# Loads of q, k pair by pair through a tile of four places, v in parts, and turning transfers behind x's transpositions

## The chip, the cores and the metric

The kernel runs on one core of one Trainium2 chip. The metric is the device time of one execution in microseconds. The core has five engines that run side by side, each in the order of its own program: TensorE (PE, with its weight loads PEld), VectorE (DVE), ScalarE (ACT), GpSimd (POOL) and SyncE (SP). SP only issues DMAs here; POOL issues all loads from HBM that change float32 into bfloat16. All DMAs run on the core's 16 DMA engines.

## The reference

Eight batches, eight heads, 576 positions, head size 64. First an attention with a decay, then a mixer along the sequence and one along the channels:

```python
scores = scale * q @ k.T                       # per batch and head, 576 x 576
cum    = cumsum(max(s, 0))
scores = where(causal, -1e9, scores + minimum(-(cum_i - cum_j), 0))
attn   = exp(scores - max) / (sum + 1e-9)
x      = (attn @ v), heads side by side        # 8 x 576 x 512
u      = x + (x.T @ U @ V).T                   # U: 576 x 32, V: 32 x 576
out    = u + max(u @ w_ch1, 0) @ w_ch2         # 512 -> 2048 -> 512
```

Inputs and output are float32; the kernel multiplies in bfloat16.

## The kernel before

**Tiling.** The 64 heads are worked in 32 pairs of heads (n = 0 to 31), four pairs to a batch (b, hp = divmod(n, 4)). For a pair the kernel needs q and k with the head size on the partitions, in a tile `slot` (one of three for the later pairs, so pair n takes over the slot of pair n - 3). `scores` multiplies k by q for the blocks on and below the diagonal into PSUM, ACT takes the exponential into a tile `pT`, DVE masks it. `values` multiplies pT by v (a column of ones beside v gives the sums), and DVE divides and writes `x_sb` (L502, L503). When the four pairs of a batch are there, `seqmix` makes u from x: products with U and V, to which DVE adds x transposed (`xT`, L547). Then `chanmix` takes 512 rows of u at a time: `hidden` (L662, ReLU by ACT at L1039) and `outputs_by_quarters` (L720), which uses a scheme of seven products in place of eight, with sums made by DVE (L698, L734).

**How q and k come.** For batches 0 to 3 (b < ZB = 4) q and k are loaded in one or a few transfers and PE transposes them (`transposes`, L322). For batches 4 to 7 the DMA transposes them: `load_pairs(b)` issues 16 loads (L121) into one of two tiles `qk_sd`, by batch in turns; `turn_pair(n)` (L358) is a transposing DMA on SP's queue that writes one of three landing places; `part_pair(n)` brings the decay rows in by two small DMAs (`rows_of`, L302) and lets DVE copy the landing into the slot (L366). `values` sends each finished pair of x to `xT` by a transposing DMA on SP as well (L510), and `by_token` does the same for u (`u_sd`, L1026). v goes by `load_v(b)` in five parts of 128 positions (the last of 64, L185) into one of the v tiles; a batch's tile is that of the batch two before it, so the load waits for the last `values` of that batch.

**The order.** A loop over n from 8 to 33, "step n" below, writes the program: loads, the turn of pair n + 3, `part_pair(n + 1)` or `transposes(n + 1)`, `scores(n)`, then `values(n - 1)`; in the second step of a batch the `seqmix` of the batch before is woven in, and in between `step_fill` puts pieces of `chanmix` at a given pace. PE and POOL keep exactly this order (the last line of the kernel ties each instruction to the one before). DVE, ACT and SP are ordered by the tile framework's scheduler after the start of the kernel, which may put an instruction ahead of where it was written: the copies of L366 stand on DVE two steps ahead of the scores that use them, right behind the scores that last used the slot, and before the change the turns stood ahead as well. Each engine then runs its own order and waits at each instruction for what it needs. POOL and SP are queues too: what waits at their head holds what is behind.

**PSUM.** Four buffers `pwork` rotate in the order of allocation between the hidden products, the output products, the tails of scores, the products of values and seqmix; two larger ones (`pscore`) take the scores. PE stops when the buffer that is next has not been read out.

Of the kernel before, what the change touches and what calls it, by code (L numbers as in the profile page):

```python
# [16 lines left out]
ALU = mybir.AluOpType  # L17


def in_program_order(tc, first, engines):  # L20

    traced, last = tc.nc.cur_bb.bb.instructions, {}
    for ins in list(traced)[first:]:
        if ins.engine not in engines:
            continue
        prev = last.get(ins.engine)
        if prev is not None:
            tc.add_manual_dep(
                ins,
                prev.name,  # L30
                mybir.DependencyInfo(
                    mybir.DependencyClass.NoSync, mybir.DependencyReason.DATA
                ),
                reason="in_program_order",
            )
        last[ins.engine] = ins


# [1 line left out]
def kernel(  # L40
# [12 lines left out]
    nc = tc.nc  # L53
    traced = len(nc.cur_bb.bb.instructions)
    E = mybir.EngineType
    B, H, S, D = q.shape
# [7 lines left out]
    NP = BH // 2  # L64
    PB = NP // B
# [5 lines left out]
    ZB = 4  # L71
    TR, RT = 96, 6
# [12 lines left out]
    def pwork():  # L85
        return ps_w.tile([128, 512], FP32, tag="w", name="pwork")
# [17 lines left out]
    qk_sd = [consts.tile([128, 2 * H * TT * D], BF16, name=f"qk_sd{i}") for i in range(2)]  # L104
    QK = 2 * PB * RT * 128
# [1 line left out]
    def alloc_qk(b):  # L107
        q_t[b], k_t[b] = qk_sd[b % 2][:TP].rearrange("p (c h x) -> c p h x", c=2, h=H)

    def by_pairs(b):  # L110
        return qk_sd[b % 2][:TR, :QK].rearrange(
            "p (hp c t two d) -> p hp c t two d", hp=PB, c=2, t=RT, two=2
        )

    def in_runs(b, h):
        return b > 2 or b == 2 and h >= 4

    def load_pairs(b):
        for h in range(H):
            for c, src in enumerate((q, k)):  # L120
                nc.gpsimd.dma_start(  # L121
                    out=by_pairs(b)[:, h // 2, c, :, h % 2, :],
                    in_=src[b, h].rearrange("(t p) d -> p t d", p=TR),
                )

    def load_qk(b, h, n):
# [44 lines left out]
    def init_v(eng, vt):  # L171
        eng.memset(vt[64:, 4, :, :], 0.0)
        eng.memset(vt[:, 0:4, :, D : D + 1], 1.0)
        eng.memset(vt[0:64, 4, :, D : D + 1], 1.0)

    def v_slot(b):
        return v_slots[b % 3 if b < 3 else 2 - b % 2]

    def load_v(b, parts=range(5)):
        vt = v_slot(b)  # L180
        if 0 < b < 3:
            init_v(nc.gpsimd, vt)
        for t in parts:
            rows_t = 128 if t < 4 else 64
            nc.gpsimd.dma_start(  # L185
                out=vt[:rows_t, t, :, 0:D],
                in_=v[b, :, ds(t * 128, rows_t), :].rearrange("h p d -> p h d"),
            )
# [40 lines left out]
    for n in range(PB):  # L229
        for hh in range(2):  # L230
            nc.sync.dma_start(
                out=slots[n][D:KA, hh, 0 : 2 * S],
                in_=rows[2 * n + hh : 2 * n + hh + 1].rearrange("n r c s -> n r (c s)"),
# [3 lines left out]
    for r, n_r, c in ((0, 3, 1), (3, 1, 0)):  # L237
        nc.sync.dma_start(
            out=rows_hbm[ds(r, n_r), ds(2 * PB, BH - 2 * PB)].rearrange("r n s -> n r s"),
            in_=rows[2 * PB :, ds(r, n_r), c, :],  # L240
# [107 lines left out]
            yield  # L348

    landings = [consts.tile([128, 2 * S], BF16, name="turned")]  # L350
    landings += [qk_sd[(ZB + i) % 2][:, ds(QK, 2 * S)] for i in range(2)]

    def landing(n):
        return landings[(n - ZB * PB) % 3]

    def turn_pair(n):
        b, hp = divmod(n, PB)
        nc.sync.dma_start_transpose(  # L358
            out=landing(n).rearrange("p (a m) -> p a m", m=TR),
            in_=by_pairs(b)[:, hp].rearrange("p c t two d -> p (c t two d)"),  # L360
        )

    def part_pair(n):
        rows_of(n)
        for hh in range(2):
            nc.vector.tensor_copy(slot_of(n)[0:D, hh, 0 : 2 * S], landing(n)[ds(hh * D, D)])  # L366
            yield
# [113 lines left out]
    def values(n, pT):  # L481
        b, hp = divmod(n, PB)
        if hp == 0:
            x_of[b] = work.tile([128, PB, 5, 128], BF16, tag="x_sb", name="x_sb")
            if b >= FT:
                xT_of[b] = work.tile([128, 4, 640], BF16, tag="xT", name="xT", bufs=1)
        x_sb, vt = x_of[b], v_slot(b)
        for hh in range(2):
            h = 2 * hp + hh
            po = pwork()[:, : 5 * (D + 1)].rearrange("p (i d) -> p i d", i=5)  # L490
            for i in range(5):
                for j in range(i + 1):
                    nc.tensor.matmul(  # L493
                        po[:, i, :],
                        lhsT=pT[:, hh, ds(place(j, i), 128)],
                        rhs=vt[:, j, h, :],
                        start=(j == 0),
                        stop=(j == i),
                        skip_group_check=True,
                    )  # L500
            rec = work.tile([128, 5, 1], FP32, tag="rec", name="rec", bufs=4)
            nc.vector.reciprocal(rec, po[:, :, D : D + 1])  # L502
            nc.vector.tensor_tensor(  # L503
                x_sb[:, hp, :, ds(hh * D, D)],
                po[:, :, 0:D],
                rec.to_broadcast([128, 5, D]),
                op=ALU.mult,
            )
            if hh == 1 and b >= FT:
                nc.sync.dma_start_transpose(  # L510
                    out=xT_of[b][:, hp, :].rearrange("p (t m) -> p t m", t=5),
                    in_=x_sb[:, hp, :, :].rearrange("p t d -> p (t d)"),
                )
            yield


# [725 lines left out]
    for n in range(2 * PB, NP + 2):  # L1242
        b, hp = divmod(n, PB)
        if hp == 0 and b + 1 < ZB:
            load(b + 1)
        if hp == (1 if b >= ZB else PB - 1) and ZB <= b + 2 < B:
            load_pairs(b + 2)
        if ZB * PB <= n + 3 < NP:
            turn_pair(n + 3)
        mixing = seqmix(b - 1) if hp == 1 and b > FT else iter(())  # L1250
        if b == B:
            fill_with(3)
            for _ in range(3):
                step(mixing)
                fill_with(2)
        if n > 2 * PB and n + 1 < NP:
            for at, _ in enumerate((transposes if n + 1 < ZB * PB else part_pair)(n + 1)):
                step_fill()
                if at == 0:
                    step(mixing)  # L1260
        if 2 * PB + 1 < n < NP:
            for at, _ in enumerate(scores(n, pT_of(n))):
                step_fill()
                if at == 1:
                    step(mixing)
        for _ in mixing:
            fill_with(1)
        if hp == 1 and FT < b < B:
            fill.append(chanmix(b - 1))
            pace[1] = 12 if b < 6 else 10  # L1270
        if 2 * PB < n <= NP:
            run(values(n - 1, pT_of(n - 1)))
        if hp == 0 and 2 <= b < B - 1:
            load_v(b + 1)
    pace[1] = 16
    while NG - 3 not in expanded:
        step_fill()
# [67 lines left out]
```

## Time and profile before

| | us |
|---|---|
| median of three runs | 357.47 (356.61 to 358.28) |
| the profiled execution, its own time | 359.33 |
| its span in the profile | 357.6 |
| PE busy, idle | 343.6, 14.0 |
| DVE, ACT, POOL busy | 264.4, 207.6, 112.6 |

The granted clock of TensorE was full all through. Times in the views are counted from the start of the span. A line of a timeline gives start, duration (several instructions may be merged into one line), engine, line of the kernel, what is written from what is read, and in brackets the idle time of the engine before it with what ended that. SPq is SP's queue: its durations are those of issuing, not of the transfer. The end of a transfer is seen in the semaphore that it raises. In PE's idle time of 14.0 us, gaps of over 0.1 us add up to 9.2 us, 2.4 of it before 23 us.

| place | where in the loop | steps |
|---|---|---|
| 65 to 104 us | batch 2 | 9 to 12 |
| 104 to 142 us | batch 3 | 13 to 16 |
| 142 to 177 us | batch 4 | 17 to 20 |
| 177 to 213 us | batch 5 | 21 to 24 |
| 213 to 248 us | batch 6 | 25 to 28 |
| 248 to 282 us | batch 7 | 29 to 32 |

(A row runs from the end of the x of one batch, L503, to that of the next; step n ends with the values of pair n - 1.)

### The profile page before, as it was taken

The page shows a single profiled execution, that of the slowest core. Times are in us where ns is not written, and L with a number is a line of the kernel's source. Part 1 is how long each engine was busy: PE and PEld are TensorE (multiplying, and loading weights), DVE is VectorE, ACT ScalarE, POOL GpSimd, SP SyncE. Part 2 cuts the span into 40 slices and gives each one's busy share as a digit, 9 for nine tenths or more (in the row PEclk, how much of TensorE's full clock was granted, in tenths as well). Part 3 has the DMA queues.
Part 4 walks back from the last instruction along what each step waited for, and adds up shares of the span by engine and source line. Part 5 has one row for each costly group of instructions (what it writes and reads, how often), then busy time and mean ns, then how long its engine had stood idle before and what let it go on. Part 6 is the DMA issues. An engine that isn't in the chain of part 4 may idle for free.

```text
span 357.6 us, 9219 instructions
## 1 busy us (share of the span) xinstructions
PE 343.6 (96%) x3770; PEld 247.9 (69%) x3770; DVE 264.4 (74%) x584; ACT 207.6 (58%) x314; POOL 112.6 (31%) x158
## 2 busy tenths in 40 slices
PE   7999999999998999999999997899899999999996
PEld 3685656665587657775678565776588558888885
DVE  8686776779789849883798465983788779676774
ACT  4786965847762577348833874347752554675710
POOL 8897274447356603850366040000000000000000
PEclk9999999999999999999999999999999999999999
DMA  6999999999999999999599999472033525010022
GB/s 100 163 193 203 177 187 121 146 144 97 192 101 171 162 168 88 167 176 159 72 120 160 204 118 90 73 163 57 0 57 83 115 30 120 29 60 31 29 90 88
DMA packets 163713, 42.06 MB, mean 118 GB/s; under 512 B 148312, under 2 KB 162040, under 8 KB 163672
## 3 DMA queue, kind: packets, MB, share of 16 engines
q0 software_dynamic: 101744, 18.45, 80.7%
q1 hardware_dynamic: 61640, 22.83, 36.0%
q8 instruction: 29, 0.48, 0.6%
q10 hardware_dynamic: 288, 0.20, 0.2%
q14 instruction: 12, 0.10, 0.1%
HBM read 37.25 MB, written 9.70 MB: 131 GB/s over the span
## 4 chain that ended last, share of the span: by engine, by line
PE 77%; DVE 12%; ACT 5%; DMA 4%; issue 2%; POOL 0%; DVEq 0%; ACTq 0%; POOLq 0%
PE pwork L662 22%; PE pwork L720 12%; PE quarter L720 9%; PE pscore L429 9%; PE pwork L493 7%; PE parts L950 6%; PE pwork L681 3%; DVE uT L547 3%; DMA xT<-x_sb 2%; ACT pT L447 2%; PE pwork L322 2%; DVE slot L345 2%; DVE o_sb L734 2%; DVE slot L698 2%; ACT hT L1039 1%
## 5 line engine op out<-in xcount | busy, mean ns | idle before, releaser
L662 PE MATMUL pwork<-uT,w_sb 128*128 128x512 bf16 x432 | 106.6, 379 | 1.1 <-ACT hT L1039 0.9
L447 ACT ACTIVATE pT<-pscore 128x1024 bf16<-128x1024 f32 x56 | 56.5, 1031 | 52.7 <-PE pscore L429 52.3
L1039 ACT ACTIVATE hT<-pwork 128x512 bf16<-128x512 f32 x108 | 65.4, 610 | 37.1 <-PE pwork L662 36.3
L662 PEld LDWEIGHTS <-w_sb 128*128 128x128 bf16 x448 | 38.7, 98 | 38.0 <-issue 1.3
L429 PE MATMUL pscore<-slot 68*128 68x320 bf16 (+1 forms) x500 | 55.4, 246 | 0.6 <-ACT hT L447 0.3
L185 POOL DMA_DIRECT2D v_slot<-in_v_dram x40 | 33.8, 860 | 67.9 <-PE pwork L493 57.6
L429 PEld LDWEIGHTS <-slot 68*128 68x128 bf16 x564 | 41.8, 97 | 18.2 <-issue 1.2
L373 DVE TENSOR_TENSOR pT<-pT,keep 128x512 bf16<-128x512 bf16 (+1 forms) x81 | 28.5, 353 | 31.7 <-ACT pT L447 28.7
L720 PEld LDWEIGHTS <-hT 128*128 128x128 bf16 x496 | 46.7, 98 | 7.5 <-issue 0.8
L493 PEld LDWEIGHTS <-pT 128*128 128x128 bf16 x870 | 32.5, 97 | 10.2 <-issue 4.4
L493 PE MATMUL pwork<-v_slot,pT 128*128 128x65 bf16 x870 | 35.8, 193 | 3.8 <-DVE uT L547 3.1
L503 DVE TENSOR_TENSOR x_sb<-pwork,rec 128x320 bf16<-128x320 f32 x64 | 31.2, 489 | 1.5
L459 ACT ACTIVATE pT<-pscore 128x1024 bf16<-128x1024 f32 x29 | 30.4, 1047 | 2.6 <-PE pscore L429 2.4
L720 PE MATMUL pwork<-w_sb,hT 128*128 128x256 bf16 x240 | 30.1, 273 | 0.3 <-DVE o_sb L734 0.3
L345 DVE COPY slot<-pwork 64x576 bf16<-64x576 bf16 x30 | 24.1, 803 | 7.2 <-PE pwork L322 6.8
L121 POOL DMA_DIRECT2D qk_sd<-in_q_dram x32 | 23.8, 743 | 14.0 <-PE pwork L322 4.9
L720 PEld LDWEIGHTS <-slot 128*128 128x128 bf16 x256 | 24.1, 98 | 5.0 <-issue 1.9
L121 POOL DMA_DIRECT2D qk_sd<-in_k_dram x32 | 23.7, 740 | 5.7 <-DMA v_slot<-in_v_dram 1.8
L720 PE MATMUL pwork<-w_sum,slot 128*128 128x256 bf16 x160 | 20.1, 273 | 1.1 <-DVE o_sb L734 1.1
L720 PE MATMUL quarter<-w_sb,hT 128*128 128x256 bf16 x144 | 18.0, 273 | 0.3 <-DVE uT L547 0.3
L681 PE MATMUL pwork<-w_sb,hT 128*128 128x512 bf16 x64 | 16.3, 379 | 0.0
L502 DVE RECIPROCAL rec<-pwork 128x5 f32<-128x5 f32 x64 | 12.0, 189 | 5.4 <-PE pwork L493 5.0
(166 smaller groups left out, 513.7 us busy)
## 6 DMA issues: line engine op xcount, KB each, us to landing
out_dram<-o_sb SPq DMA_DIRECT2D x34, 256.0 KB
v_slot<-in_v_dram POOLq DMA_DIRECT2D x32, 128.0 KB, 7.7
w_sb<-in_moe_w_ch_dram POOLq DMA_DIRECT2D x4, 1024.0 KB, 13.3
qk_sd<-in_q_dram POOLq DMA_DIRECT2D x32, 72.0 KB, 6.0
qk_sd<-in_k_dram POOLq DMA_DIRECT2D x32, 72.0 KB, 5.9
qk_sd<-in_q_dram POOLq DMA_DIRECT2D x4, 288.0 KB, 12.4
qk_sd<-in_k_dram POOLq DMA_DIRECT2D x4, 288.0 KB, 11.5
qk_sd<-in_q_dram POOLq DMA_DIRECT2D x4, 144.0 KB, 5.2
```

Of the source, the lines that this page charges most:

```text
L121: nc.gpsimd.dma_start(out=by_pairs(b)[:, h // 2, c, :, h % 2, :], in_=src[b, h].rearrange("(t p) d -> p t d", p=TR),)
L185: nc.gpsimd.dma_start(out=vt[:rows_t, t, :, 0:D], in_=v[b, :, ds(t * 128, rows_t), :].rearrange("h p d -> p h d"),)
L345: copies(n, hh, par)(in_turn[:, :, :, :, par], src.rearrange("p c t m -> p c m t"))
L373: nc.vector.tensor_tensor(dst, dst, keep[:, :, 0:w].to_broadcast([128, n_tiles, w]), op=ALU.min)
L429: nc.tensor.matmul(dst, lhsT=slot[0:KA, hh, ds(S + j * 128, 128)], rhs=slot[0:KA, hh, lo:hi], start=True, stop=True,)
L447: nc.scalar.activation(pT[:, hh, 0:1024], near, EXP, scale=scale)
L459: nc.scalar.activation(pT[:, :, 1024:1536], mid.rearrange("p (a b) -> p a b", a=2), EXP, scale=scale)
L493: nc.tensor.matmul(po[:, i, :], lhsT=pT[:, hh, ds(place(j, i), 128)], rhs=vt[:, j, h, :], start=(j == 0), stop=(j == i), skip_group_check= ...
L503: nc.vector.tensor_tensor(x_sb[:, hp, :, ds(hh * D, D)], po[:, :, 0:D], rec.to_broadcast([128, 5, D]), op=ALU.mult,)
L662: nc.tensor.matmul(f1, lhsT=w1_sb[:, kt, ds(nf * 128, 128)], rhs=u[:, kt, :], start=(kt == 0), stop=(kt == 3),)
L720: nc.tensor.matmul(acc[:, i, :], lhsT=a[:, kt, ds(i * 128, 128)], rhs=b[:, kt, :], start=(begin and i == 0 and kt == 0), stop=(kt == HF - ...
L1039: nc.scalar.activation(hT[:, nf, :], f1, RELU)
```

## The change

Three things are changed, for batches 4 to 7:

1. q and k of a pair are loaded by themselves (`load_pair(n)`, four transfers), all into the first of the two `qk_sd` tiles, which has four places, one for each n % 4. The four pairs of batch 4 are still loaded together, in step 11; after that step n loads pair n + 7, whose place is that of pair n + 3, so the load waits for the turn of that pair, which the same step issues. Before, batches 5, 6 and 7 were loaded whole in steps 15, 17 and 21, into the two tiles in turns. One of the three landing places moves to the start of the second tile.
2. The five parts of v for batches 4 to 7 are spread over the four steps of the batch before: two, one, one, one. Before, all five stood in the first of these steps.
3. Each turn gets a tie to the last transposition of x that was written before it (`after`), so that it stands behind it in SP's order. When `turn_pair(n + 3)` is written in step n, that is the one of pair n - 2. No semaphore is added for it.

```diff
+def after(tc, ins, prev):
+    tc.add_manual_dep(
+        ins,
+        prev.name,
+        mybir.DependencyInfo(mybir.DependencyClass.NoSync, mybir.DependencyReason.DATA),
+        reason="in_program_order",
+    )
...
-    def by_pairs(b):
-        return qk_sd[b % 2][:TR, :QK].rearrange(
-            "p (hp c t two d) -> p hp c t two d", hp=PB, c=2, t=RT, two=2
+    def of_pair(n):
+        return qk_sd[ZB % 2][:TR, ds(n % PB * QK // PB, QK // PB)].rearrange(
+            "p (c t two d) -> p c t two d", c=2, t=RT, two=2
         )
...
-    def load_pairs(b):
-        for h in range(H):
+    def load_pair(n):
+        b, hp = divmod(n, PB)
+        for hh in range(2):
             for c, src in enumerate((q, k)):
                 nc.gpsimd.dma_start(
-                    out=by_pairs(b)[:, h // 2, c, :, h % 2, :],
-                    in_=src[b, h].rearrange("(t p) d -> p t d", p=TR),
+                    out=of_pair(n)[:, c, :, hh, :],
+                    in_=src[b, 2 * hp + hh].rearrange("(t p) d -> p t d", p=TR),
                 )
...
-    landings += [qk_sd[(ZB + i) % 2][:, ds(QK, 2 * S)] for i in range(2)]
+    landings += [qk_sd[ZB % 2][:, ds(QK, 2 * S)], qk_sd[(ZB + 1) % 2][:, 0 : 2 * S]]
...
+    x_turned = []
+
+    def last_sp():
+        return [ins for ins in list(nc.cur_bb.bb.instructions) if ins.engine == E.SP][-1]
+
     def turn_pair(n):
-        b, hp = divmod(n, PB)
         nc.sync.dma_start_transpose(
             out=landing(n).rearrange("p (a m) -> p a m", m=TR),
-            in_=by_pairs(b)[:, hp].rearrange("p c t two d -> p (c t two d)"),
+            in_=of_pair(n).rearrange("p c t two d -> p (c t two d)"),
         )
+        after(tc, last_sp(), x_turned[-1])
...
+                x_turned.append(last_sp())
...
-        if hp == (1 if b >= ZB else PB - 1) and ZB <= b + 2 < B:
-            load_pairs(b + 2)
         if ZB * PB <= n + 3 < NP:
             turn_pair(n + 3)
+        if n + 5 == ZB * PB:
+            for m in range(ZB * PB, (ZB + 1) * PB):
+                load_pair(m)
+        if (ZB + 1) * PB <= n + 7 < NP:
+            load_pair(n + 7)
...
-        if hp == 0 and 2 <= b < B - 1:
-            load_v(b + 1)
+        if 2 <= b < B - 1:
+            if b + 1 < ZB:
+                load_v(b + 1, range(5 if hp == 0 else 0))
+            else:
+                load_v(b + 1, ((0, 1), (2,), (3,), (4,))[hp])
```

More of the change, by code (lines that the diff above doesn't have):

```diff
@@ L27, in in_program_order @@
         if prev is not None:
[L28 to L35, printed above, removed]
+            after(tc, ins, prev)
         last[ins.engine] = ins
```

## The prediction

> **What bounds it now.** I read the page first, then the table of windows, the chain that ended last, and the timelines of PE, DVE, SyncE (SP) and GpSimd (POOL) around the one long DMA in that chain.
>
> ```profile
> PE 343.6 (96%) x3770; PEld 247.9 (69%) x3770; DVE 264.4 (74%) x584; ACT 207.6 (58%) x314; POOL 112.6 (31%) x158
> DMA  6999999999999999999599999472033525010022
> q0 software_dynamic: 101744, 18.45, 80.7%
> q1 hardware_dynamic: 61640, 22.83, 36.0%
> ```
>
> PE is busy for 343.6 of 357.6 us, at clock 9 in every slice: only about 14 us of idle PE can be gained at all. The DMA engines are near full until about 223 us.
>
> ```profile
> 214.58 8.62 DMA xT<-x_sb
> ```
>
> ```profile
> 211.86 2.62 SPq L358 DMA_TRANSPOSE qk_sd<-qk_sd  x1
> 214.58 1.23 SPq L510 DMA_TRANSPOSE xT<-x_sb  x1
> ```
>
> ```profile
> 210.97 4.21 POOL L185 DMA_DIRECT2D v_slot<-in_v_dram  x5 [14.32 <-PE pwork L493]
> ```
>
> ```profile
> 223.29 0.76 DVE L547 TENSOR_TENSOR uT<-pwork,xT 128x192 bf16<-128x192 f32 x2 [3.27 <-DMA xT<-x_sb]
> ```
>
> ```profile
> 224.10 0.61 PE L493 MATMUL pwork<-v_slot,pT 128*128 128x65 bf16 x15 [2.83 <-DVE uT L547]
> 226.83 1.91 PE L720 MATMUL pwork<-w_sum,slot 128*128 128x256 bf16 x16 [0.78 <-DVE o_sb L734]
> ```
>
> This is the only place where a DMA holds PE after the start. The transposition of x of pair 23 (xT 23 below) is issued at 214.58, behind five parts of v and one turning transfer, takes 8.62 us, DVE waits 3.27 us, PE 2.83 + 0.78. In the same place of batches 3 and 4 the last gap is 0.30 (before L720 at 149.86 and 185.46), so 2.83 + 0.48 = **3.3 us** hangs on it.
>
> The second thing to see is where the copies of turned q, k stand on DVE, in a quiet step:
>
> ```profile
> 160.48 0.49 DVE L503 TENSOR_TENSOR x_sb<-pwork,rec 128x320 bf16<-128x320 f32 x1
> ...
> 165.93 0.94 DVE L366 COPY slot<-turned 64x1152 bf16<-64x1152 bf16 x2 [0.58 <-PE pwork L429]
> 166.99 0.22 DVE L373 TENSOR_TENSOR pT<-pT,keep 128x128 bf16<-128x128 bf16 x1
> 167.13 0.19 DVE L502 RECIPROCAL rec<-pwork 128x5 f32<-128x5 f32 x1
> 167.35 0.49 DVE L503 TENSOR_TENSOR x_sb<-pwork,rec 128x320 bf16<-128x320 f32 x1
> ```
>
> ```profile
> 156.54 5.15 SPq L1026 DMA_TRANSPOSE u_sd<-uT  x1
> 161.79 0.53 SPq L744 DMA_DIRECT2D out_dram<-o_sb  x1
> 162.41 0.94 SPq L302 DMA_DIRECT2D slot<-rows_hbm  x2
> 163.57 2.21 SPq L358 DMA_TRANSPOSE qk_sd<-qk_sd  x1
> 165.88 2.14 SPq L510 DMA_TRANSPOSE xT<-x_sb  x1
> ```
>
> The copy at 165.93 is that of pair 22 and waits for the scores of pair 19, which had its slot: DVE's program has it two steps ahead of its use. x of pair 17 ended at 160.97.
>
> **Part 1: turns behind x's transpositions.** In the built order of the two programs PE, ACT and DVE are the same instruction for instruction; only SP and POOL differ. On SP each turn k (16 to 31) now stands straight behind xT k-5; before, turns ran one to three steps earlier (turns 16 and 17 were issued at 86.35 and 95.57, their copies ran at 109.34 and 122.91). The gain: xT 23 now goes ahead of turn 28. It can go when x ends, 212.82, with four q, k loads and one part of v ahead. A load took 0.72 us of POOL per issue and 5.9 us to land (page, part 6), so xT 23 should land by 212.9 + 5.9 = 218.8, before DVE is ready for it at 220.03. Saved: **3.3**. The bounds are 0 (it still lands at 223) and 3.6 (both gaps whole).
>
> The cost: copy k heads DVE's queue at its old place, behind it stand the last mask and the x of the step, and PE needs that PSUM buffer back. In the step shown x's first half ends at 167.84, and PE takes the buffer four allocations on, by the second group of the x8 of L662 from 167.52, that is at 168.38: DVE may be **0.54** late before PE stops. In the step with seqmix (copies 16, 20, 24) DVE runs without a break into gaps that PE already has, so its room there is 0.
>
> When turn k lands: xT's issue, plus 1.4 for xT's own issue (1.23 and a register step), plus the turn's latency. No view prints that latency; the trace's updates of the turns' semaphores, last update less issue, give for the sixteen turns 3.30, 3.36, 3.38, 3.40 and 3.44 when no load was in flight, and otherwise 4.22, 4.66, 4.95, 5.50, 5.52, 5.92, 6.02, 7.43, 9.01, 9.44, 9.71. The long ones had five parts of v or a u_sd ahead. In the changed kernel the loads of pair k+4 wait for turn k (they overwrite its place), so at each turn there are about four q, k loads and a part of v under way, never sixteen and five: I take **4.2**, the row with least ahead of it; 3.4 after the long step (copies 17, 21, 25) and for 29 to 31, when no q, k is loaded; the bounds are 3.4 and 5.0 (between 4.66, with q, k alone ahead, and 5.50).
>
> xT 13, 17 and 21 also stand behind u_sd on SP, which issued for 4.6, 5.15 and 5.7 us there but 3.19 and 1.93 at 236.66 and 276.24, without loads. I take 4.0 (the one at 88.88 took 4.01). From u_sd's start at 121.30, 157.5 and 194.96 that, an out of 0.6 and, for the first two, a pair of row loads of 0.94 let xT go at 126.9, 163.0 and 199.6; bounds 2.0 and as before.
>
> Wait of PE = xT's issue + 1.4 + latency - copy's old start - room, all in the old times:
> - 16: 104.68 + 5.6 - 109.34 - 0 = 0.9
> - 18: 126.9 + 5.6 - 130.44 - 0.54 = 1.5
> - 19: 133.03 + 5.6 - 137.92 - 0.54 = 0.2
> - 20: 141.76 + 5.6 - 146.14 = 1.2
> - 22: 163.0 + 5.6 - 165.93 - 0.54 = 2.1
> - 24: 177.0 + 5.6 - 181.77 = 0.8
> - 26: 199.6 + 5.6 - 201.55 - 0.54 = 3.1
> - 27: 204.15 + 5.6 - 209.03 - 0.54 = 0.2
> - 29, 30, 31: 228.70, 234.70, 241.60 + 4.8 - 232.76, 238.54, 245.16 - 0.54 = 0.2, 0.4, 0.7
> - 17, 21, 23, 25, 28: none (23 and 28 have copies 7.7 and 14 us behind x)
>
> The sum is **11.3**; with 3.4 and u_sd at 2.0 it is 2.2, with 5.0 and u_sd as before 19.5.
>
> **Part 2: loads pair by pair, v in parts.** The same q, k and v issues by POOL (0.72 and 0.89 us each); POOL's queue hides them, since nothing but loads stands in it. POOL now waits at each pair for turn m-4, and the last part of v of a batch stands behind such a pair. The part of batch 5: turn 22 lands at about 168.6, four loads issue until 171.6, the part until 172.5, landing 7.7 later (page) at 180.2; PE needs it at 186.3. Cover 6 us, so 0; a turn later than that by more would cost its excess. Pairs are loaded four steps before their turn (about 35 us against 5.9), so no turn waits for its load. For batch 7 no pair load separates the parts of v any more; turn 28 takes that, with 14 us of room. Cost 0.
>
> At each landing the copies on DVE and the next pair's issue on POOL now start together. Copies beside POOL issues took 0.71, 0.57, 0.71 and 0.69 at 109 to 124, but 0.45 at 146.14 and 181.77, as long as those alone (0.45 to 0.46): I take 0; the bound is 24 copies x 0.26 = 6.2. [...]
>
> **Sum.** 11.3 - 3.3 = **+8.0**, on the profiled execution 359.33 (span 357.6 and 1.7 around it). That execution is 1.9 above the median of the runs; I put the difference on the median: 357.47 + 8.0 = **365.5**.
>
> **Rivals.**
> - The copies' room is larger than I read, or turns behind xT are all quiet: no new wait, only 3.3 is gained: **354.2**. For it: five turns at 3.4. Against: the engines near full. It decides at a latency of 3.4 with u_sd at 2.0, where 2.2 of waits are left and the time is 356.4.
> - Turns wait behind the loads that the last turn released, at 5.0 and more: 357.47 + 19.5 - 3.3 = **373.7**. For it: the 4.66 and 5.50 rows; in steps of 7.5 us the circle copy, x (2.5), xT (1.4), turn (5.0) is 8.9.
> - The change does not free xT 23, as the five parts of v of batch 7 are still released by the same values and follow each other: 3.3 stays, **368.8**. Against: pair 31's issues stand before them on POOL.
> - The copies lose to POOL's issues as at 109 to 124: 365.5 + 6.2 = **371.7**.
>
> **How the numbers follow.** Forecast with waits of about 4 to 15 us 0.50, the long turns 0.12, xT 23 not freed 0.09, the copies 0.05: together 0.76 and slower. Waits that about eat the gain, 0.10: within 0.5% (1.8 us, about what a measurement of this kernel can tell from no change). The first rival 0.14: faster. The range 356.0 to 374.0 leaves out the first rival and a tail beyond the second, about 2 in 10; the forecast's own range is 359 to 371.
>
> **What would show it.** Right: DVE idle before L366 released by DMA (turned or qk_sd), most at copies 18, 22, 26 and 20; PE idle before L662 and L720 released by DVE x_sb or uT; the 3.27 before L547 near 220 gone; xT 23 landing in under 6 us. Wrong: L366 still released by PE L429 everywhere. A wait of PE at L493 for v_slot would make the v parts the cause.

## The result, and the profile after

| | before | changed |
|---|---|---|
| median of six executions, us | 357.42 (356.61 to 359.57) | 389.26 (387.13 to 391.75) |
| profiled execution, its span | 359.33, 357.6 | 389.2, 387.5 |
| PE busy, idle | 343.6, 14.0 | 355.2, 32.3 |
| mean granted clock of TensorE | 1.0 | 0.969 |

The ratio is 1.0888 (95% interval 1.0839 to 1.0937). The direction was forecast, the size was not: 365.5 was predicted, with a range up to 374.0. The span grew by 29.9 us, of which 18.3 are idle time of PE and 11.6 are PE's busy time for the same 3770 matmuls.

The page of the changed kernel (line numbers are about 9 higher than before: copies of turned q, k are L374, turns L365, x's transposition L518, x L511, the sums for u L556, `hidden` L671, `outputs_by_quarters` L729):

```profile
PE 355.2 (92%) x3770; PEld 253.7 (65%) x3770; DVE 264.0 (68%) x584; ACT 207.9 (54%) x314; POOL 113.6 (29%) x158
...
PEclk9999999999998989789996998999999999999999
...
PE 48%; DMA 28%; DVE 11%; issue 5%; POOL 3%; ACT 2%; SPq 2%; DVEq 0%; POOLq 0%; ACTq 0%
DMA qk_sd<-qk_sd 11%; PE quarter L729 9%; PE pwork L671 9%; DMA turned<-qk_sd 8%; PE pwork L729 6%; PE parts L959 5%; PE pwork L501 4%; DMA qk_sd<-in_q_dram 4%; PE pscore L437 4%; PE pwork L690 3%; DMA qk_sd<-in_k_dram 3%; POOL qk_sd L124 3%; DVE uT L556 2%; DVE o_sb L743 2%; DVE x_sb L511 2%
```

Two things are new. The turns (DMA from `qk_sd` to `qk_sd` or `turned`) are on the chain that ended last with 19% of the span, where before no turn stood. And the clock digits fall to 6, 7 and 8 in the middle, in the stretch in which the turns run. What waits for the turns is seen in the waits of DVE and, behind them, of PE in the changed kernel (us in total, times, longest):

```profile
DVE slot L374 <- DMA qk_sd<-qk_sd: 22.6, 8, 5.9
DVE slot L374 <- DMA turned<-qk_sd: 9.8, 5, 4.2
```

```profile
PE pwork L671 <- DVE x_sb L511: 13.6, 5, 4.6
PE pwork L601 <- DVE uT L556: 8.7, 3, 3.7
```

One such place, step by step, is copy 18. The timelines of SP, DVE and PE in the changed kernel:

```profile
128.76 1.23 SPq L518 DMA_TRANSPOSE xT<-x_sb  x1
130.17 2.26 SPq L365 DMA_TRANSPOSE qk_sd<-qk_sd  x1
```

```profile
132.24 0.43 DVE L381 TENSOR_TENSOR pT<-pT,keep 128x512 bf16<-128x512 bf16 x1 [0.98 <-ACT pT L455]
137.80 0.94 DVE L374 COPY slot<-qk_sd 64x1152 bf16<-64x1152 bf16 x2 [5.14 <-DMA qk_sd<-qk_sd]
138.77 0.23 DVE L381 TENSOR_TENSOR pT<-pT,keep 128x128 bf16<-128x128 bf16 x1
138.91 0.19 DVE L510 RECIPROCAL rec<-pwork 128x5 f32<-128x5 f32 x1
139.13 0.49 DVE L511 TENSOR_TENSOR x_sb<-pwork,rec 128x320 bf16<-128x320 f32 x1
```

```profile
134.84 1.03 PE L671 MATMUL pwork<-uT,w_sb 128*128 128x512 bf16 x4
139.68 1.89 PE L671 MATMUL pwork<-uT,w_sb 128*128 128x512 bf16 x4 [3.82 <-DVE x_sb L511]
141.36 1.06 PE L437 MATMUL pscore<-slot 68*128 68x128 bf16 x6
```

xT 13 (the transposition of x of pair 13) goes when x ends, the turn of pair 18 straight behind it, landing 7.51 us after its issue. The copy stands on DVE with the mask and the x of the step behind it; DVE is idle for 5.14 us, and PE stops for 3.82 us since the PSUM buffer that it needs is read out by that x. Behind the stop the same four products take 1.89 us instead of 1.03. That second loss is the clock. The table of windows of the changed kernel around the stop (a row gives the stretch, its length, the busy time and the instructions of PE, PEld, DVE, ACT and POOL, then the granted clock, the DMA share and GB/s):

```profile
132.80:136.20 3.40, 3.06 (x42) 1.74 (x40) 0.00 (x0) 2.37 (x5) 0.00 (x0) 1.00 1.83 89
136.20:139.60 3.40, 0.00 (x0) 0.00 (x0) 1.71 (x6) 0.30 (x1) 1.36 (x2) 1.00 0.27 38
139.60:143.00 3.40, 3.32 (x12) 1.52 (x13) 1.34 (x5) 1.14 (x2) 2.29 (x4) 0.50 1.42 115
143.00:146.40 3.40, 3.40 (x31) 1.97 (x30) 2.62 (x5) 3.19 (x5) 0.00 (x0) 0.99 1.93 126
```

In the stretch behind the stop PE works all the time at clock 0.50 and gets 12 matmuls done; in the next, at full clock, 31. The trace records half clock in five places of the changed kernel, 3.41 us or twice that long: from 115.7, 139.6, 160.1, 204.5 and 231.8, together 23.9 us. PE was busy for 21.4 of these, so 10.7 us of work at full clock were lost, which is most of the 11.6 that its busy time grew.

The eight stops of over 0.5 us behind late copies, in the order of the prediction:

| copy | stop predicted | turn, issue to landing | DVE waits | PE stops |
|---|---|---|---|---|
| 16 | 0.9 | 5.21 | 1.99 | 1.91 |
| 18 | 1.5 | 7.51 | 5.14 | 3.82 |
| 20 | 1.2 | 5.91 | 3.20 | 3.07 |
| 22 | 2.1 | 6.28 | 4.23 | 2.91 |
| 24 | 0.8 | 6.68 | 3.32 | 3.74 |
| 26 | 3.1 | 5.69 | 5.89 | 4.58 |
| 30 | 0.4 | 3.25 | 2.36 | 2.18 |
| 31 | 0.7 | 3.26 | 2.06 | 0.93 |
| sum | 10.7 | | | 23.1 |

(Copy 31 made two stops, 0.71 and 0.22 us. The sum predicted is 11.3 with the small ones at 19, 27 and 29.)

The gain came too: xT 23 is issued at 242.32, lands 6.0 us later, neither DVE nor PE waits for it, and where before PE stopped for 2.83 and 0.78 us it now stops once:

```profile
252.94 1.25 PE L729 MATMUL pwork<-w_sum,slot 128*128 128x256 bf16 x10 [0.41 <-DVE o_sb L743]
```

### The profile page after: what moved, and what is told of

Its sections match the earlier page's. It is cut to its first block, busy times and chain, and to the rows that moved or that the text cites. A ratio compares the mean times of both kernels' runs of the same rounds, so it can differ in the third digit from the quotient of the medians.

```text
span 387.5 us, 9203 instructions
## 1 busy us (share of the span) xinstructions
PE 355.2 (92%) x3770; PEld 253.7 (65%) x3770; DVE 264.0 (68%) x584; ACT 207.9 (54%) x314; POOL 113.6 (29%) x158
## 4 chain that ended last, share of the span: by engine, by line
PE 48%; DMA 28%; DVE 11%; issue 5%; POOL 3%; ACT 2%; SPq 2%; DVEq 0%; POOLq 0%; ACTq 0%
DMA qk_sd<-qk_sd 11%; PE quarter L729 9%; PE pwork L671 9%; DMA turned<-qk_sd 8%; PE pwork L729 6%; PE parts L959 5%; PE pwork L501 4%; DMA qk_sd<-in_q_dram 4%; PE pscore L437 4%; PE pwork L690 3%; DMA qk_sd<-in_k_dram 3%; POOL qk_sd L124 3%; DVE uT L556 2%; DVE o_sb L743 2%; DVE x_sb L511 2%
## 5 line engine op out<-in xcount | busy, mean ns | idle before, releaser
L671 PE MATMUL pwork<-uT,w_sb 128*128 128x512 bf16 x432 | 109.7, 386 | 14.6 <-DVE x_sb L511 13.6
L671 PEld LDWEIGHTS <-w_sb 128*128 128x128 bf16 x448 | 39.0, 99 | 54.0 <-DVE x_sb L511 16.2
L437 PE MATMUL pscore<-slot 68*128 68x320 bf16 (+1 forms) x500 | 56.3, 248 | 0.6 <-ACT hT L455 0.3
L729 PEld LDWEIGHTS <-hT 128*128 128x128 bf16 x496 | 47.1, 99 | 7.9 <-issue 0.8
L501 PEld LDWEIGHTS <-pT 128*128 128x128 bf16 x870 | 34.9, 101 | 7.7 <-issue 1.4
L501 PE MATMUL pwork<-v_slot,pT 128*128 128x65 bf16 x870 | 38.0, 198 | 0.9 <-DVE slot L348 0.6
L511 DVE TENSOR_TENSOR x_sb<-pwork,rec 128x320 bf16<-128x320 f32 x64 | 31.2, 488 | 1.5
L729 PE MATMUL pwork<-w_sb,hT 128*128 128x256 bf16 x240 | 31.2, 279 | 0.3 <-DVE o_sb L743 0.3
L729 PEld LDWEIGHTS <-slot 128*128 128x128 bf16 x256 | 24.9, 101 | 5.1 <-issue 1.5
L374 DVE COPY slot<-qk_sd 64x1152 bf16<-64x1152 bf16 x20 | 9.1, 453 | 23.3 <-DMA qk_sd<-qk_sd 22.6
L729 PE MATMUL pwork<-w_sum,slot 128*128 128x256 bf16 x160 | 21.8, 287 | 0.6 <-DVE o_sb L743 0.6
L729 PE MATMUL quarter<-w_sb,hT 128*128 128x256 bf16 x144 | 18.0, 273 | 0.3 <-DVE uT L556 0.3
```

The costliest lines, as they stand in the source:

```text
L437: nc.tensor.matmul(dst, lhsT=slot[0:KA, hh, ds(S + j * 128, 128)], rhs=slot[0:KA, hh, lo:hi], start=True, stop=True,)
L501: nc.tensor.matmul(po[:, i, :], lhsT=pT[:, hh, ds(place(j, i), 128)], rhs=vt[:, j, h, :], start=(j == 0), stop=(j == i), skip_group_check= ...
L511: nc.vector.tensor_tensor(x_sb[:, hp, :, ds(hh * D, D)], po[:, :, 0:D], rec.to_broadcast([128, 5, D]), op=ALU.mult,)
L671: nc.tensor.matmul(f1, lhsT=w1_sb[:, kt, ds(nf * 128, 128)], rhs=u[:, kt, :], start=(kt == 0), stop=(kt == 3),)
L729: nc.tensor.matmul(acc[:, i, :], lhsT=a[:, kt, ds(i * 128, 128)], rhs=b[:, kt, :], start=(begin and i == 0 and kt == 0), stop=(kt == HF - ...
```

## The experiments

Theory A: the tie is the whole cause. It makes turns land after the place that their copies have on DVE; DVE waits there in order, PE stops for its PSUM buffers, and where a stop is long the clock halves behind it. Rival B: the DMA traffic is the cause: the loads that each turn releases (part 2) fill the DMA engines. In the later runs rival B says this as well: the clock falls with the traffic and not with the stops. In each run "before" was measured beside it; ratios are against that.

### The tie alone, and all but the tie

The changed kernel without its tie:

```diff
-        after(tc, last_sp(), x_turned[-1])
```

> The changed kernel without the tie of each turn to x's transposition; loads pair by pair and v in parts stay. Theory A (the tie makes the turns land after the place that their copies have on DVE; DVE stops, PE stops behind it, and TensorE's granted clock is halved for 3.4 or 6.8 us after the longer stops): with turns issued when the scheduler likes, no copy waits for a DMA, the clock stays at 1.0, and the time is 354 to 358 us. Rival B (the loads that each turn's landing releases fill the DMA engines and are what delays the turns; the tie costs little): copies go on waiting, and the time stays above 370.

The kernel before with the tie for all turns, loads and v as before:

```diff
             in_=by_pairs(b)[:, hp].rearrange("p c t two d -> p (c t two d)"),
         )
+        after(tc, last_sp(), x_turned[-1])
...
                 )
+                x_turned.append(last_sp())
```

> The kernel before with the tie alone; loads by batch as before. Theory A: copies of turned q, k wait for DMAs at most of the sixteen pairs, the clock falls to 0.5 in several stretches, and the time is 370 to 395 us. Rival B: within 1% of before, 354 to 361.

| | us | ratio to before | span, clock of the profile |
|---|---|---|---|
| all but the tie | 356.13 | 0.9990 [0.9961, 1.0019] | 354.0, 0.998 |
| the tie alone | 387.40 | 1.0843 [1.0807, 1.0879] | 386.3, 0.968 |

Without the tie the copies never wait for a DMA; in the list of what released them (changed kernel without the tie) only PE is left:

```profile
  PE pwork L436: 3.9, 9
```

With the tie alone the whole loss is there, clock included. The stops lie elsewhere (PE in the kernel before with the tie):

```profile
117.84 0.39 PE L608 MATMUL pwork<-V_end,ux 128*128 128x64 bf16 x4 [5.33 <-DVE uT L563]
...
133.59 1.04 PE L678 MATMUL pwork<-uT,w_sb 128*128 128x512 bf16 x4 [1.29 <-DVE x_sb L518]
```

Copies 16, 20 and 24 now cost 5.33, 5.47 and 5.72 us, the other stops 1.1 to 1.8. In these three steps all five parts of v are issued beside the turn, which lands after 8.53, 8.00 and 8.68 us; the others take 3.2 to 4.9 (7.62 for turn 28). With part 2 the turns of 18, 22 and 26 are longer instead: 7.51, 6.28 and 5.69 us in the changed kernel, 4.30, 4.63 and 3.90 here. Whether the parts of v or the loads of q and k by pair do that was not taken apart. So part 2 moves the stops about, and their sum stays: PE is idle for 32.3 us in both. Rival B falls for the loads.

### The copies moved, the tie kept

The changed kernel, each copy tied on DVE behind the DVE instruction written before it; SP and the loads are as in the changed kernel.

```diff
+            last = [i for i in list(nc.cur_bb.bb.instructions) if i.engine == E.DVE][-1]
             nc.vector.tensor_copy(slot_of(n)[0:D, hh, 0 : 2 * S], landing(n)[ds(hh * D, D)])
+            after(tc, [i for i in list(nc.cur_bb.bb.instructions) if i.engine == E.DVE][-1], last)
```

> The changed kernel whole, with each copy of turned q, k tied on DVE behind the last x written before it, which puts it 4 us or more later in DVE's order; nothing else moves. Theory A: the turns have landed by then, no copy waits, DVE's 3.27 us wait for the transposition of x of pair 23 is gone as well, and the time is 354 to 356, below before. Rival B: the turns are late for their scores too, PE waits at the scores instead, above 365.

353.54 us (353.10 to 356.32), ratio 0.9907 [0.9873, 0.9942]: 0.9% below before, and far below the changed kernel. The engines of this version, and its DVE from copy 21 (first line) to copy 22 (last line):

```profile
PE 342.7 (98%) x3770; PEld 248.1 (71%) x3770; DVE 263.8 (75%) x584; ACT 207.4 (59%) x314; POOL 113.0 (32%) x158
```

```profile
166.15 0.91 DVE L375 COPY slot<-qk_sd 64x1152 bf16<-64x1152 bf16 x2
...
171.40 0.69 DVE L709 TENSOR_TENSOR slot<-slot,hT 128x1024 bf16<-128x1024 bf16 x1
172.01 0.44 DVE L375 COPY slot<-turned 64x1152 bf16<-64x1152 bf16 x1
```

The turns are as long as in the changed kernel (3.25 to 7.03 us; turn 22 lands at 169.29), but copy 22 now stands some 6 us later in the work and finds its turn landed. No copy waits for a DMA, after the first microseconds no stop is over 1 us, and the clock stays full (in one of six executions, the longest, its mean was 0.989). A rival is that moving the copies changed PE's own waits. By the traces it did not: PE's 7540 instructions (products and weight loads) wait for the same engines in both kernels, except for one product and its weight load in `outputs_by_quarters` near 223 us. So the late turns cost nothing by themselves; they cost through the early place of the copies. This shows the middle step of theory A directly.

Two more versions of the kernel before take it apart: the tie and the late copies without part 2, and the late copies alone.

> The kernel before with the ties of the turns behind x's transpositions and the copies moved behind the DVE work written before them; loads of q, k by batch and all parts of v at once, as before. If the loads by pair and the parts of v are worth nothing, as I costed them: the same 353.5 as with all three parts and late copies. If they matter: turn 28 behind xT 23, and xT 23 behind five parts of v, so part of the 3.3 us at 221 would be back, up to 356.

> The kernel before with the copies moved behind the DVE work written before them, and nothing else. Theory A: the early place of the copies costs before nothing, as no copy waits there for a DMA and PE's room covers them; the stop at 221 stays, time as before, 356 to 357. If the place of the copies is worth something by itself: below 355.5.

They took 353.84 (0.9935 [0.9912, 0.9958]) and 353.88 us (0.9937 [0.9915, 0.9960]). The last expectation missed: the later place of the copies is worth 2.2 us without any tie, and with it neither the tie nor part 2 shows a gain of its own. Where it comes from is seen in part: the five stops of 0.23 to 0.34 us in the seqmix steps (at 112.6, 113.9, 149.0, 184.0 and 184.6 in the profile of the next experiment, 1.5 us in all) are one of 0.32 in the version with all three, and two of 0.51 and 0.48 with the late copies alone. The rest, of the size of the interval, stays open.

### The tie where the gain was meant to be

The kernel before with the tie for turn 28 alone.

```diff
+        if n == 28:
+            after(tc, last_sp(), x_turned[-1])
```

> The kernel before with the tie for the one turn of pair 28, which before stood ahead of the transposition of x of pair 23 and whose copy has 14 us of room. Theory A: x of pair 23 lands before DVE needs it, the 2.83 us stop of PE near 221 goes and no other comes, 354 to 355. Rival B (five parts of v released at the same time hold it, whichever way the turn stands): the stop stays, 357 to 358.

355.58 us, ratio 0.9962 [0.9945, 0.9980], a little above what was expected. The stop of 2.83 is gone, 0.60 of the second is left:

```profile
223.09 1.91 PE L737 MATMUL pwork<-w_sum,slot 128*128 128x256 bf16 x16 [0.60 <-DVE o_sb L751]
```

The gain is 1.4 us and not 3.3. The reason is in the other profiles: in the changed kernel without the tie, turn 28 stands ahead of xT 23 as before, and yet PE stops there for 0.66 us only. xT 23 lands at 219.55 there and at 219.45 with turn 28 tied, which is no difference. (The turn that stands straight ahead of xT 23, issued at 211.86 in the profile of before, is that of pair 30; it stays ahead in both.) The stop of 2.83 belongs to the one execution of before that I worked from, which was 1.9 above the median. In the profiles of the next two sections, of kernels that leave this place as it was, the same stop took between nothing and 2.47 us. So the 1.4 us are measured, but that they come from xT 23 is not shown.

### A DVE that is late without any DMA

If theory A is right, any delay of DVE in that place should stop PE, and long ones should halve the clock. I tried to make it late in the kernel before, at copies 18, 22 and 26, with no DMA moved. First by repeating the first copy, four and twelve more times:

```diff
+            for _ in range(5 if hh == 0 and n in (18, 22, 26) else 1):
+                nc.vector.tensor_copy(slot_of(n)[0:D, hh, 0 : 2 * S], landing(n)[ds(hh * D, D)])
```

> The kernel before with the first copy of turned q, k of pairs 18, 22 and 26 made four more times: 4 x 0.455 = 1.8 us more on DVE at three places, no DMA changed. DVE may be 0.54 late before PE stops, so PE should stop 1.3 us at each: + 3.8, 361.2 us. Theory A with the clock: stops this short leave the granted clock at 1.0.

> The same with twelve more copies: 5.5 us more on DVE at three places, PE stops of 4.9 us each, 14.8 in sum. If a stop costs only its length: 372.2 us and clock 1.0 throughout. If a long stop also halves the granted clock: three stretches of 3.4 us at 0.5, each 1.7 us more, 377.3; with 6.8 each 382.4.

The first took 356.45 (1.0000 [0.9976, 1.0024]), the second 362.16 (1.0155 [1.0116, 1.0194]), clock full in both profiles (0.995 and 0.994 in two executions of the second). Both expectations missed. The repeated copies did not stay together: masks and x of the step stand between them on DVE, so x was late by a little only; in the second PE had many stops, but behind the first microseconds none over 2.1 us. Next came one long instruction in their place, ahead of the copies:

```diff
+            if hh == 0 and n in (18, 22, 26):
+                src = landing(n)[ds(0, D)].rearrange("p (o x) -> p o x", o=1)
+                nc.vector.tensor_reduce(
+                    slot_of(n)[0:D, 0, 0:1],
+                    src.to_broadcast([D, 4, 2 * S]),
+                    axis=mybir.AxisListType.XY,
+                    op=ALU.max,
+                )
```

> The kernel before, with one long DVE instruction right ahead of the copies of pairs 18, 22 and 26 (a maximum over the landing, read twice, written to a place of the slot that the copy then overwrites): about 2.4 us each, so DVE is late by that in three places, while no DMA, no load and no turn moves. With 0.54 us of room PE should stop for about 1.9 us in each place, 5.6 us in all. Theory A (a stop costs its length, and TensorE's clock halves after it only where the stop is long, as 1.91 us of idle in a window did not do it in the changed kernel): granted clock stays 1.0, time about 5.6 above before, 362. If any stop halves the clock for a window of 3.4 us: 1.7 more for each, 367. Rival B (the clock fell because of the DMA traffic): clock 1.0 here and in the next run.

> The same with the landing read four times: about 4.8 us, stops of about 4.2 us, 12.8 us in all. Theory A: after each stop the granted clock is 0.5 for one or two windows of 3.4 us, which costs 1.7 us each: 5 to 10 us more, so 18 to 23 above before, about 377. Rival B (the clock fell because of the DMA traffic, which is that of before here): clock 1.0, about 12.8 above before, 369.

356.04 (1.0011 [0.9985, 1.0037]) and 355.90 us (0.9987 [0.9964, 1.0010]): nothing, against both expectations. The instruction needs only the first head's scores, so it began 4 us ahead of the copy, in time in which DVE had been idle. Placed between the two copies it can't do that:

```diff
+            if hh == 1 and n in (18, 22, 26):
+                src = slot_of(n)[0:D, 0, 0 : 2 * S].rearrange("p (o x) -> p o x", o=1)
+                nc.vector.tensor_reduce(
+                    slot_of(n)[0:D, 1, 0:1],
...
```

> The kernel before, with a long DVE instruction of about 2.5 us between the two copies of pairs 18, 22 and 26 (a maximum over the first copy, read twice; its result is overwritten by the second copy). It stands right ahead of the last mask and the x of the step, where a copy that waits for its turn holds DVE in the changed kernel; no DMA moves. DVE is 2.5 late there, less 0.45 for the second copy, which now goes behind, less 0.54 of room: stops of PE of about 1.5 us in three places, 4.5 in all. Theory A: the granted clock stays at 1.0 and the time is about 4.5 above before. Rival B (the clock fell because of the DMA traffic): the same here.

> The same with about 4.95 us in each place: stops of PE of about 4 us, 12 in all. Theory A: the granted clock is 0.5 for one window of 3.4 us or more behind each stop, 1.7 us each, so about 17 or more above before. Rival B (the clock fell because of the DMA traffic): clock 1.0, about 12 above before.

The first took 355.95 (0.9996 [0.9973, 1.0019]), the second 361.79 us (1.0142 [1.0104, 1.0180]); both expectations missed. DVE and PE of the second:

```profile
135.78 0.45 DVE L374 COPY slot<-qk_sd 64x1152 bf16<-64x1152 bf16 x1 [0.58 <-PE pwork L437]
136.26 4.95 DVE L368 TENSOR_REDUCE slot<-slot 64x1 bf16<-64x4608 bf16 x1
...
141.48 0.89 DVE L511 TENSOR_TENSOR x_sb<-pwork,rec 128x320 bf16<-128x320 f32 x2
```

```profile
99.70 1.01 PE L437 MATMUL pscore<-slot 68*128 68x128 bf16 x6 [2.03 <-DMA slot<-rows_hbm]
100.52 1.89 PE L670 MATMUL pwork<-uT,w_sb 128*128 128x512 bf16 x4
...
137.37 1.89 PE L670 MATMUL pwork<-uT,w_sb 128*128 128x512 bf16 x8
139.10 0.61 PE L437 MATMUL pscore<-slot 68*128 68x128 bf16 x6
139.54 1.03 PE L670 MATMUL pwork<-uT,w_sb 128*128 128x512 bf16 x4
140.41 0.61 PE L437 MATMUL pscore<-slot 68*128 68x128 bf16 x6
```

DVE is held for 4.95 us in the very place where the changed kernel waits for turn 18. From the first copy to x it takes 5.70 us instead of the 1.42 of an undisturbed step (165.93 to 167.35 before), so x is 4.3 us late, against 4.6 in the changed kernel; and from 137 to 147 us PE does not stop at all. The order of PE's instructions is unchanged, but what they wait for is not: in the built program (before on the left, this one on the right) the products of `hidden` in these steps take other PSUM buffers, whose last readers are on ACT:

```
L662 Ldweights w_sb [waits DVE]                | L670 Ldweights w_sb
L662 Matmult pwork<-uT,w_sb 128x512 [waits PE] | L670 Matmult pwork<-uT,w_sb 128x512 [waits Activation]
```

I read this so: the tile framework gives out the PSUM buffers by the times that it plans; a delay that it knows, as that of a long instruction, it works around, and the landing of a turn, 3.25 to 9.5 us behind its issue in the changed kernel, it does not know. In the changed kernel and in the one with the tie alone PE waits for the same engines in the same places as before: by the traces none of its 7540 instructions differs. In the two kernels with the long instruction between the copies, 9 and 28 of them differ, all in the steps of these three copies and behind them. That the other buffers are what kept PE going was not tested by itself. The upper two lines of PE show one thing more (this execution took 367.61 us, the longest of five): a stop that no copy made, for a small load of decay rows, and half clock behind it (0.50 in the windows from 99.5 to 106.3); four products take 1.89 us. What makes the 5.3 us of the median was not followed up.

### Single stops of different lengths

So the stops had to be made by late turns. Each of four kernels is the kernel before with the tie for one turn (`if n == 16:` and so on, as for turn 28 above).

> The kernel before with the tie for turn 16 alone; loads and v as before. With all turns tied and these loads PE stopped 5.33 us for copy 16. Theory A (a stop of PE, and the half clock that follows it, are the whole cost): a stop of about 5 us and one or two windows of 3.4 us at half clock, 1.7 to 3.4 more, so 7 to 8.5 above before, 363 to 365. Rival B (the clock falls with the DMA load of the whole middle part): clock 1.0 with one stop, 5 above before.

> The tie for turn 18 alone. With all turns tied PE stopped 1.29 us for copy 18 with these loads, and 3.82 with the loads by pair. Theory A: a stop of 1 to 2 us, too short to halve the clock: 357.5 to 358. Rival B: the same.

> The tie for turn 22 alone. With all turns tied the copy of pair 22 waited for PE and not for its turn with these loads, as xT 17 and its turn had landed. Theory A: no stop, time as before, 356.3. If turn 22 comes late here (xT 17 stands behind u_sd): up to 2 us of stop, 358.5.

> The tie for turn 26 alone. With all turns tied PE stopped 1.20 us for copy 26 with these loads; my prediction had 3.1 us there. Theory A: a stop of 1 to 3 us; the granted clock stays 1.0 up to 1.6 us and is halved for a window above 2: 357.5 to 361.

| tied turn | us | ratio to before | stop of PE | half clock in the profile |
|---|---|---|---|---|
| 26 | 357.73 | 1.0037 [1.0000, 1.0073] | 1.83 | none |
| 18 | 360.54 | 1.0122 [1.0050, 1.0195] | 2.73 | none |
| 22 | 364.24 | 1.0210 [1.0162, 1.0257] | 3.77 | 6.83 |
| 16 | 363.89 | 1.0196 [1.0149, 1.0244] | 5.82 | 6.83 |

PE of the kernels with turn 18 and with turn 22 tied:

```profile
135.13 1.04 PE L679 MATMUL pwork<-uT,w_sb 128*128 128x512 bf16 x4 [2.73 <-DVE x_sb L519]
```

```profile
172.12 1.89 PE L679 MATMUL pwork<-uT,w_sb 128*128 128x512 bf16 x4 [3.77 <-DVE x_sb L519]
173.80 1.06 PE L445 MATMUL pscore<-slot 68*128 68x128 bf16 x6
174.67 1.89 PE L679 MATMUL pwork<-uT,w_sb 128*128 128x512 bf16 x4
```

The granted clock of the kernel with turn 22 tied, in stretches of 3.4 us (columns as above):

```profile
163.90:167.30 3.40, 3.40 (x47) 2.18 (x45) 0.42 (x1) 3.09 (x6) 0.00 (x0) 1.00 1.20 176
167.30:170.70 3.40, 1.05 (x11) 0.32 (x7) 0.45 (x1) 0.96 (x2) 0.00 (x0) 1.00 0.78 157
170.70:174.10 3.40, 1.98 (x7) 0.88 (x8) 1.87 (x6) 0.06 (x1) 0.00 (x0) 0.50 0.47 88
174.10:177.50 3.40, 3.40 (x17) 1.71 (x15) 0.43 (x1) 2.21 (x4) 0.00 (x0) 0.50 0.24 47
177.50:180.90 3.40, 3.40 (x33) 1.94 (x32) 2.24 (x4) 3.10 (x5) 0.00 (x0) 1.00 0.02 2
```

One late turn, all else as before, and the clock falls right behind its stop and nowhere else. Behind a stretch with 2.35 us of idle PE it is 0.50, while the DMA engines move less (88 and 47 GB/s there, 176 and 157 ahead of it). Rival B falls for the clock as well. A stop of 2.91 us of the changed kernel, from 182.7 to 185.6, did not halve it: of the windows of 3.41 us that its clock's steps mark (last section), the two in which this stop lies, from 180.59 and 184.00, had 1.27 and 1.64 us of idle time, and the clock stayed at 1.00. The price of the stop with turn 22 tied: 3.77 us and half of the 5.4 us that PE was busy at half clock, 2.7, make 6.5; measured were 7.7 (5.8 to 9.2). For turn 16 it is 5.82 + 2.7 = 8.5 against 7.4 (5.3 to 8.7).

The kernel with turn 18 tied is a case between 2 and 3 us. Its four executions took 359.11 and 359.43 us at a mean clock of 1.0, 361.65 at 0.995 and 364.12 at 0.989: the same program, and the clock falls in some executions and not in others. The profiled one, with 2.73 us of stop and full clock, is 2.9 above before, just the stop; how long the stop was in the others no profile shows. With turn 26 tied, eight of ten executions had a clock of 0.998 or more (357.15 to 358.20 us), two 0.995 and 0.994 (360.37 and 361.11).

For the 1.6 and 2 us in the expectation for 26, the changed kernel has a window with 1.64 us of idle PE that left the clock full and one with 2.21 that did not. Two of the four expectations missed: no stop was expected for turn 22 (xT 17 goes 3.5 us after its x, behind u's transposition on SP, and the turn lands at 170.1), and one too short to halve the clock for 18. The expectation for 22 rested on a misreading. In the kernel with the tie alone the profile names PE as what ended the wait of copy 22. But its turn landed there at 185.72 us and the copy began at 185.81, with the same 0.09 us between the two as at most other late copies: it did wait for its turn.

## The prediction, step by step

- **That turns behind x's transposition come late for their copies.** Right, and it is the cause: all but the tie 356.13, the tie alone 387.40, and with the copies moved 353.54 us.
- **Which copies stop PE.** Right: 16, 18, 20, 22, 24 and 26 are the large ones in both lists, nothing at 17, 21, 23, 25, and 19, 27 and 29 stay small. Only 30 is out of line (below).
- **The latency of a turn, 4.2 us, bounds 3.4 and 5.0.** This is the first term that was mis-sized. The turns of the six large copies took 5.21 to 7.51 us, 6.2 on average, above even the upper bound. I took the row with least ahead of it and left out the long ones, as those with "five parts of v or a u_sd ahead". That row was not one of "four q, k loads and a part of v under way": the turn issued at 132.03 in before had no load in flight any more, the last had landed at 131.32. In the changed kernel the turns of 19, 23 and 27 had the loads that I named ahead of them, and took 4.6 to 5.0. The six large copies had more. For 16, 20 and 24 two parts of v were issued beside the turn, as the change itself has it in the first step of a batch; for 18, 22 and 26 u_sd went up to 6.2 us ahead, with the loads behind it. Each of the six turns landed 0.1 to 1.7 us behind the part of v issued last before it or with it; turn 18 was issued 0.6 us behind that part. No run tells apart which of these transfers does it. 2.0 us more for each of six copies is 12 us; their stops came to 20.0 instead of 9.6. In part the difference is made up by the term for u_sd on SP, which took 2.20 and 2.43 us ahead of xT 13 and 17 instead of 4.0 (3.89 ahead of xT 21).
- **The sums.** The sum for copy 22 starts u_sd at 157.5 and gives no reason, where the line shown has 156.54; with that its stop would be 1.2 instead of 2.1. And the same working with 5.0 and u_sd as before gives 21.2 and not 19.5, so that the rival with long turns would stand at 375.4. Neither changes the account.
- **The room of 0.54 us.** About right: at copies 18, 22 and 26 PE's stop is 0.74 us shorter than the copy's lateness (5.14 less the 0.58 that it waited for PE anyway, less 3.82). That 16, 20 and 24 have next to none is right too.
- **Copies 29 to 31.** The turns took the forecast 3.25 to 3.5; but the stops at 30 and 31 were 2.18 and 0.93 instead of 0.4 and 0.7. From the end of x to where copy 30 stands DVE took 3.05 us (262.30 to 265.35) instead of 3.61 before, as work that had waited for other engines was there at once, and SP was 0.6 us slower for xT. I had taken the distances of before, which lateness shortens.
- **The gain of 3.3 us.** xT 23 does land in time with the tie, but without it as well (219.55 us). The size came from one execution 1.9 us above the median, and I put the difference on the median: the tie of turn 28 alone gains 1.4 us (0.7 to 2.0).
- **Part 2 at 0.** Right for its loads: no wait of PE for v, and no turn waits for its load. That some turns are longer with it (18, 22 and 26: 7.51, 6.28 and 5.69 us instead of 4.30, 4.63 and 3.90 with the tie alone) belongs to the latency; with the tie alone and all parts at once the idle time of PE is the same.
- **Copies beside POOL's issues at 0.** Right: the 20 copies from `qk_sd` took 427 to 456 ns with each turn's landing starting four issues, and the 12 from `turned` at most 602. The bound of 6.2 us did not show. What grew is the time of POOL's issues: after 100 us the 17 issues of q and k by POOL that ran beside a copy took 732 to 911 ns, the 31 others 725 to 739. That costs nothing here, as no turn waits for its load.
- **The clock.** A term that was missing: 10.7 to 11.6 us. I read "at clock 9 in every slice", put the clock at nothing and did not ask what stops of 1 to 4 us would do to it. In the changed kernel the clock was at half for 3.41 us or its double, each time behind a window of 3.41 us in which PE had been idle for 2.21 us or more. With turn 18 tied the same program had a mean clock of 1.0 in two executions and of 0.995 and 0.989 in two.

Together: stops of 23.1 and 11.6 of clock, less 3.2 at xT 23 and 1.6 of small stops that only before had (0.6 of it in the first 6 us), are the 29.9 us of the span. The rival with long turns, 373.7, was the nearest; it fell 15.6 us short, 11.6 of them the clock.

## What to carry to other kernels

Before a transfer is put behind another in a queue, look up where the instruction that consumes it stands on its engine: if a scheduler has pulled that one ahead of work that is urgent, the delay is paid by all that stands behind it, and moving the consumer (here 389 to 353.5 us) was worth more here than the order of the queue. If my reading of the trial delays is right, a wait that the framework can't foresee gets no buffers planned around it, and a delay that it can foresee is no model of it. A stop of TensorE can cost more than its length (a program that stopped for 2.73 us in its profile cost 2.6 to 7.6 in four executions, one with 3.77 cost 7.7), and the size of a stop that is to be removed should not be taken from a single execution.

## What the runs showed of the hardware

- In the changed kernel the five stretches of half clock lasted 3.41 us or twice that, and their starts are 7, 6, 13 and 8 times 3.41 us apart. Counted on windows of 3.41 us that these steps mark, half clock followed windows in which PE was idle for 2.21, 2.31 and 2.70 us and, twice, throughout, and not those with 1.91, 1.64, 1.27 and 1.10. With turn 22 tied it followed a stretch of 3.40 us with 2.35 of idle PE, with turn 16 tied one of 3.50 us that was idle throughout, and with the long instruction of 4.95 us one of 3.50 us with 2.00 (from 96.0). The runs do not show where between these the bound lies, nor that idle time alone sets it.
- Once halved, it stayed so for a second window where the first had 0.95 and 1.24 us of idle PE in the changed kernel, 1.42 and 1.40 with turn 22 and turn 16 tied, and 0.20 with the long instruction of 4.95 us. In the changed kernel it returned to full behind windows with 0.00 to 0.19.
- In the changed kernel a turn took 3.25 to 3.5 us where no load was issued in the 6 us ahead of it. With four loads of q, k and one part of v issued up to 3.5 us ahead it took 4.6 to 5.0; with a u_sd besides, some 6 us ahead, 5.7 to 7.5; with two parts of v just ahead or beside it 5.2 to 6.7; and with five 9.5 (turn 28).
- In the changed kernel, after 100 us, POOL's issues of q and k loads took 725 to 739 ns, and up to 911 ns where a DVE copy of 64x1152 ran beside them; the copies kept their 0.45 us, one took 0.60.
